# Order and engines of the last sums: an attention and gated feed-forward kernel on one core

## The chip, the cores and the metric

The kernel runs on one core of one Trainium2 chip. The metric is the device time of one execution in microseconds (us); a time is the median of several runs. The engines are named as in the profile: PE is TensorE (PEld its weight loads), DVE is VectorE, ACT is ScalarE, POOL is GpSimd and SP is SyncE, which issues most of the DMAs.

## The reference

Two blocks follow one another. The first is attention with a threshold: of each row of scores only those within `tau` of the row's maximum are kept. The second is a gated feed-forward block on the attention's output, with its heads put side by side. All data are float32.

```python
# q, k, v: (8, 8, 576, 64) = batch, heads, sequence, head size; tau = 0.02
scores = matmul(q, k^T) / sqrt(64)
scores = where(scores >= max(scores) - tau, scores, -1e9)
attn   = exp(scores - max(scores)); attn = attn / (sum(attn) + 1e-9)
x      = matmul(attn, v)            # -> (8 * 576 = 4608 tokens, 512)

# w_gate, w_val: (512, 1536); w_out: (1536, 512)
g   = x @ w_gate
out = (g * sigmoid(g) * (x @ w_val)) @ w_out
```

## The kernel before

**Work and stages.** The 64 pairs of batch and head are taken two heads at a time. From the second batch on, such a pair is a segment of three slots (`slot_scores`, `slot_rest`, L2042 and L2063). A slot computes 6 tiles of 128 x 288 scores, takes maxima, exponentials and masks with row sums, adds the halves of each sum (`exchange` on ACT, L2115; `total` on DVE, L2120 and L2121, which leaves the reciprocal `ri`), scales the six tiles (on ACT, L2133, or, for as many as the table `POOLED` says, on POOL, L2130) and transposes them (DVE, L2135). `attend` (L2141) multiplies a segment's three slots with the values (PE, L2157), one slot after the next segment begins. The feed-forward block runs on units of 512 tokens (one batch, of which 64 tokens per batch are put aside; those of all batches make up the last unit). In the code a unit is `c`, and `B` = 8: `c` = B - 1 is the last batch's unit, `c` = B that of the tokens put aside.

**Products by sums.** Every matrix product of the block is done by Strassen's scheme with seven products in place of eight, most of them nested twice. So each needs sums of its operands (`inner_sums`, `early`, `late`, `second_of_s1`: SBUF to SBUF, through `dve_tt`, L929, or `pool_tt`, L926) and sums of its results (`fold`, `folded`, `combine`, `add`).

**Behind the last scores.** Once the last slot is done, `tail[0]` is set and the kernel goes through four stages. (1) The rest of unit B - 2's output products (`px` and `py`, L1768), with the last `attend` between its fifth and sixth. (2) The gates: for each of six columns `g` and each of the units B - 1 and B one `Whole` (L2526) of seven products, `p1`, `p5`, the former one's `p4`, `p2`, `p6`, `p3`, `p7` (PE, L2543). Behind `p6` two fills copy a result from PSUM (ACT, L1271 and L1273); `p7` waits for them. Behind `p3` and `p7` DVE adds the results (L2615, L2625) and POOL folds them (`fold`, four instructions); `finish` takes the tanh of the fold (ACT, L2593), multiplies on DVE (L2595) and then on DVE or POOL. The next `p4` waits for L2625. (3) The output products of unit B - 1 (`Deep`): the steps `p1`, `gates_end` (the last `Whole`'s `p4`), `p2`, `p7_alone`, `p5_flat`, `p6_alone`, `p3_flat`, `p4_alone`. (4) Those of unit B: `p1`, `gates_end`, `p7_alone`, `p2`, and so on: here the seventh product stands ahead of the second. What stage (4) reads was stored in `hall_hbm` (L2608) and is loaded by four DMAs of SP (L2669).

**Sums around the change.** In `Deep`, `early` begins the sums `s3` and `s1` over the halves of the gated values; `second_of_s1` adds one more behind the last value of column 4; `late` adds the last of `s1` and the three of `s2`, each 128 x 512. `inner_sums(o, ...)` makes four sums of 128 x 384 for the nested product `o`: `o` = 1 is the second product's operand, 5 the sixth's, 6 the seventh's.

**What sets the order.** The order on each engine is fixed when the program is built, by a planner (`Plan`, L28). Every piece is a job with an engine, a cost in us, a rank and the jobs it depends on. `peek` (L60) takes the engine that can start first and, among the jobs that are ready there, the lowest rank, then the earliest ready:

```python
n = min((i for i, j in enumerate(jobs) if j.ready <= start + (0.0 if j.rank else self.PATIENCE)),
        key=lambda i: (self.rank(jobs[i], start), jobs[i].ready, i))
```

`PATIENCE` is 0.2 and holds for rank 0 alone; a job of rank 0 that is ready up to 0.2 later is taken before one of rank 1. `lag` is time between the end of a job on its engine and the moment its result counts as there. PE's products are issued in the order of the code.

Of the kernel before, what the change touches and what calls it, by code (L numbers as in the profile page):

```python
# [14 lines left out]
ALU = mybir.AluOpType  # L15
# [129 lines left out]
def kernel(  # L145
# [13 lines left out]
    B, H, S, D = q.shape  # L159
# [1101 lines left out]
    class Seven(Buf):  # L1261
# [13 lines left out]
        def fold(self, eng, rank, *deps):  # L1275

            y = self.place.rearrange("p (x q) -> p x q", q=P)
            tt, took, less = (dve_tt, 0.36, 0.23) if eng == "DVE" else (pool_tt, 0.85, 0.52) if tail[0] else (pool_tt, 0.75, 0.44)
            twice = lambda x: y[:, x:x + 1].broadcast_to((P, 2, P))
            j = job(eng, took, tt(y[:, 1:3], twice(0), y[:, 1:3], ALU.add), *deps, rank=rank)  # L1280
            j = job(eng, took, tt(y[:, 0:7:6], twice(2), y[:, 5:7], ALU.add), j, rank=rank)
            j = job(eng, less, tt(y[:, 2], y[:, 0], y[:, 3], ALU.add), j, rank=rank)
            return job(eng, took, tt(y[:, 4:6], twice(6), y[:, 4:6], ALU.add), j, rank=rank)

    class Flat:

# [388 lines left out]
    class Deep:  # L1675
# [37 lines left out]
            self.sixth_place = xall[:, 2 * KW:3 * KW]  # L1713
            self.sixth_sums(mark)

        by_pool = False

        def second_of_s1(self):
            self.by_pool = True
            x = NF2 // 2 - 2  # L1720
            self.ready["s1"].append(self.sum(self.a21, self.a21, self.a22, ALU.add, x, self.ready["s3"][x], gated[self.c, 1, NF2 - 2]))

# [10 lines left out]
        def sum(self, out, a, b, op, x, *deps, rank=2):  # L1733
            fs = slice(2 * x, 2 * x + 2)
            tt, eng, took = (dve_tt, "DVE", 0.62) if tail[0] else (pool_tt, "POOL", 1.3)
            rank = min(rank, 1) if tail[0] else rank
            if self.by_pool and not self.in_outputs:
                tt, eng, took = pool_tt, "POOL", 1.3
            return job(eng, took, tt(out[:, fs], a[:, fs], b[:, fs], op), *deps, rank=rank)

        def inner_sums(self, o, a, place, ready, *deps):

            a11, a21, a12, a22 = quarters(a)
            flat = place if len(place.shape) == 2 else place.rearrange("p f n -> p (f n)")
            s1, s2, s3, s4 = (flat[:, n * QW:(n + 1) * QW].rearrange("p (f q) -> p f q", q=P) for n in range(4))
            tt, eng, took = (dve_tt, "DVE", 0.55) if tail[0] else (pool_tt, "POOL", 1.0)
            rank = 0 if o == 1 and self.c == B - 1 else 0 if o == 1 else 1 if o == 5 or o in (3, 6) and not tail[0] or o in (0, 6) and tail[0] or self.c == B - 2 else 2
            j3 = job(eng, took, tt(s3, a11, a21, ALU.subtract), *ready, *deps, rank=rank)
            j1 = job(eng, took, tt(s1, a21, a22, ALU.add), *ready, *deps, j3, rank=rank)
            j2 = job(eng, took, tt(s2, s1, a11, ALU.subtract), j1, rank=rank)  # L1750
            j4 = job(eng, took, tt(s4, a12, s2, ALU.subtract), j2, rank=rank)
            self.inner[o] = [(a11, ready), (a12, ready), (s4, [j4]), (a22, ready), (s1, [j1]), (s2, [j2]), (s3, [j3])]
# [310 lines left out]
    def slot_rest(seg, t, pss, mark, pooled, max_by_act, rank):  # L2063
        m = 2 * NU3
        mx, nm, th, ri, tot = statistics("mx", "nm", "th", "ri", "tot")
        sm = sums[0]
        sums.rotate(1)
        old_sums, sum_users[0] = sum_users[0], []
        sum_users.rotate(-1)
        tiles = [(h, u) for u in range(NU3) for h in range(2)]  # L2070
        at_of = lambda h, u: seg["p"] + (2 * (NU3 * t + u) + h) * SH
        scs = {(h, u): pss[h][:, u, 0:SH] if u < 2 else pss[h][:, :, SH:SH + SQ] for h, u in tiles}
        flat = {x: pall[:, at_of(*x):at_of(*x) + SH] for x in tiles}
        ps = {x: y if x[1] < 2 else y.rearrange("p (a n) -> p a n", a=2) for x, y in flat.items()}
        n_of = lambda h, u: NU3 * h + u
        rs = []
        for h, tile_ in enumerate(pss):
            n = n_of(h, 0)
            rs.append(job("DVE", 0.72, lambda n=n, tile_=tile_: nc.vector.tensor_reduce(  # L2079
                out=mx[:, n:n + 2, 0], in_=tile_[:, :, 0:SH], axis=AX.X, op=ALU.max, negate=True), mark, rank=0))  # L2080
            rs.append(job("DVE", 0.42, lambda n=n, tile_=tile_: nc.vector.tensor_reduce(  # L2081
                out=mx[:, n + 2:n + 3, 0], in_=tile_[:, :, SH:SH + SQ], axis=AX.XY, op=ALU.max, negate=True), mark, rank=0))

        def largest():
            for g in range(NG):
                o = g ^ 1
                nc.vector.tensor_reduce(out=mx[g * G:(g + 1) * G, 0:m, 1], in_=mx[o * G:(o + 1) * G, 0:m, 0:1], axis=AX.X, op=ALU.max)
            nc.vector.tensor_reduce(out=nm[:, 0:m], in_=mx[:, 0:m, :], axis=AX.X, op=ALU.min)

        def others():  # L2090
            for g in range(NG):
                o = g ^ 1
                nc.scalar.copy(mx[g * G:(g + 1) * G, 0:m, 1], mx[o * G:(o + 1) * G, 0:m, 0])

        if max_by_act:
            oj = job("ACT", 0.78, others, *rs, rank=0)
            nj = job("DVE", 0.18, lambda: nc.vector.tensor_reduce(out=nm[:, 0:m], in_=mx[:, 0:m, :], axis=AX.X, op=ALU.min), oj, rank=0)
        else:
            nj = job("DVE", 0.82, largest, *rs, rank=0)
        ej = job("ACT", 0.25, lambda: nc.scalar.activation(th[:, 0:m], nm[:, 0:m], AF.Identity, bias=cut, scale=-1.0), nj, rank=0)  # L2100
        masks = {}
        for h, u in tiles:
            x, n = (h, u), n_of(h, u)
            ej = job("ACT", 0.42, lambda x=x, n=n: nc.scalar.activation(ps[x], scs[x], AF.Exp, bias=nm[:, n:n + 1]), ej,  # L2104
                     masks.get((h, u - 1)), rank=0)
            masks[x] = job("DVE", 0.45, lambda x=x, n=n: nc.vector.scalar_tensor_tensor(  # L2106
                out=ps[x], in0=scs[x], scalar=th[:, n:n + 1], in1=ps[x], op0=ALU.is_ge, op1=ALU.mult, accum_out=sm[:, n, 0:1]),
                ej, *old_sums, rank=0)
        sc_users[:] = masks.values()
        behind_scores[0] = rs[0]  # L2110

        def exchange():
            for g in range(NG):
                o = g ^ 1
                nc.scalar.copy(sm[g * G:(g + 1) * G, 0:m, 1], sm[o * G:(o + 1) * G, 0:m, 0])  # L2115

        xj = job("ACT", 0.78, exchange, *masks.values(), rank=1)

        def total():
            nc.vector.tensor_reduce(out=tot[:, 0:m], in_=sm[:, 0:m, :], axis=AX.X, op=ALU.add)  # L2120
            nc.vector.reciprocal(out=ri[:, 0:m], in_=tot[:, 0:m])  # L2121

        rj = job("DVE", 0.36, total, xj, rank=1)
        sum_users[-1].append(rj)
        for u in range(NU3):
            scaled = []
            for h in range(2):
                x, n = flat[h, u], n_of(h, u)
                if h and u < pooled:
                    scaled.append(job("POOL", 0.48 if seg["i"] >= 3 * NP else 0.4, lambda x=x, n=n: nc.gpsimd.tensor_scalar(  # L2130
                        out=x, in0=x, scalar1=ri[:, n:n + 1], scalar2=1.0, op0=ALU.mult, op1=ALU.mult), rj, rank=1))
                else:
                    scaled.append(job("ACT", 0.46, lambda x=x, n=n: nc.scalar.activation(x, x, AF.Copy, scale=ri[:, n:n + 1]), rj, rank=rank))  # L2133
            both = pall[:, at_of(0, u):at_of(0, u) + 2 * SH]
            seg["turned"].append(job("DVE", 0.72, lambda both=both: nc.vector.transpose(out=both, in_=both), *scaled, rank=rank))  # L2135
# [139 lines left out]
    GV = {1: 3, 2: 6, 3: 4, 4: 6, 5: 7, 6: 3, 7: 5, 8: 7, 9: 0}  # L2275
    GV_FIRST = {1: 5, 2: 8, 3: 2, 4: 5, 5: 7, 6: 2, 7: 5, 8: 7, 9: 0}
    CH = {0: 2, 1: 3, 10: 4, 11: 4}
    POOLED = {0: 3, 1: 1, 2: 1, 3: 3, 4: 3, 5: 2, 6: 1, 7: 2, 8: 1}
    MAX_BY_ACT = (0, 1, 3, 4, 5, 6, 8, 9)
    FIRST_POOLED = {0: 2, 4: 1, 5: 1, 8: 1, 9: 1, 11: 2, 12: 2, 13: 3, 15: 3, 16: 3, 17: 2, 19: 2, 20: 2, 22: 3, 23: 3}  # L2280
    FIRST_MAX_BY_ACT = (1, 3, 6, 9, 10, 11, 12, 13, 14, 18, 20, 21)
# [56 lines left out]
    for s, (n, x) in enumerate((n, x) for n in range(len(halved)) for x in range(NU3)):  # L2338
# [20 lines left out]
            store_last(0, j)  # L2359
        if s == 1:  # L2360
            prepare_v(seg)
        at_, pooled, max_by_act = (kk, POOLED, MAX_BY_ACT) if b > DEEP else (s, FIRST_POOLED, FIRST_MAX_BY_ACT)
        slot_rest(seg, t, pss, mark, pooled.get(at_, 0), at_ in max_by_act, 1 if x == NU3 - 1 else 2)
        if x == 1 and n > 0:
            for place, load in held:
# [270 lines left out]
    for g in range(NF2):  # L2636
        for c in (B - 1, B):
# [10 lines left out]
            for fn in (new.p2, new.p6, new.p3, new.p7) if old is not None else (new.p5, new.p2, new.p6, new.p3, new.p7):  # L2648
                fn()
                if (c, g) == (B, NF2 - 1) and fn == new.p2:  # L2650
                    state["deep"].sums_of_last(plan.t + plan.PIPE)
                if (c, g) == (B, NF2 - 1) and fn == new.p6:
                    state["deep"].late(plan.t + plan.PIPE)
            old = new
    state["last_product"] = old.p4
    begin_outputs(B - 1)
# [56 lines left out]
```

## Time and profile before

| | |
|---|---|
| median of 3 runs | 1343.5 us (1342.71 to 1345.19) |
| the profiled execution | 1344.29 us; its span, first to last instruction, 1342.4 us |
| PE | busy 1327.0 us (99%), granted clock 0.999 |
| DVE | busy 1082.9 us (81%) |
| ACT | busy 899.1 us (67%) |
| POOL | busy 932.8 us (69%) |
| last scores on PE | from 1110.45 us |
| last `attend` | from 1126.85 us |
| first product of the gates | from 1136.26 us |
| first output product of unit B - 1 | from 1267.05 us |
| first output product of unit B | from 1303.63 us |
| end of PE's last product, about | 1338.8 us |

In a timeline a row is: start, length, engine, line, operation, output from inputs with shapes, count, and in brackets the idle time of the engine before it and what released it. Rows of one line and shape that follow each other are merged, and an instruction's length includes what it waits for inside. In the view of waits a row is: who waited for whom, us in total, times, longest.

### The profile page before, as it was taken

The numbers are of one execution on the slowest core, as the hardware profiler recorded it, in microseconds if no ns is written. First come the engines' busy times: TensorE is split into PE (matmuls) and PEld (weight loads), VectorE is DVE, ScalarE is ACT, GpSimd is POOL, SyncE is SP. The second block draws the span as 40 slices with busy tenths as digits, with TensorE's granted clock in tenths as the row PEclk, the third lists the DMA queues.
The fourth block names the chain that finished last, engine by engine and source line by source line (L and its number), as shares of the span: only waits on it lengthen the run. The fifth ranks groups of instructions, "written<-read, shape, count | busy, mean of one in ns | idle before, by whom it ended". The sixth has DMA issues, their size and how long they took to land. (4 is left out here: it accounts for less than half of the span.)

```text
span 1342.4 us, 41686 instructions
## 1 busy us (share of the span) xinstructions
PE 1327.0 (99%) x16274; PEld 1123.1 (84%) x16274; DVE 1082.9 (81%) x2891; ACT 899.1 (67%) x2341; POOL 932.8 (69%) x1115
## 2 busy tenths in 40 slices
PE   9999999999999999999999999999999999999998
PEld 7777877787887878888888888888888889999998
DVE  7888898888887778888888887888888887667886
ACT  6888777767756677787777777777777775344300
POOL 2688497565685759857895779677976799856720
PEclk9999999999999999999999999999999999999999
DMA  8852424356557553656365746655474627565241
GB/s 180 205 188 92 85 58 134 122 150 178 154 166 220 174 167 89 208 165 219 76 201 168 232 111 187 178 168 149 115 214 146 213 68 232 158 202 183 88 169 40
DMA packets 230884, 209.81 MB, mean 156 GB/s; under 512 B 167968, under 2 KB 185376, under 8 KB 223008
## 3 DMA queue, kind: packets, MB, share of 16 engines
q1 hardware_dynamic: 226768, 206.22, 52.2%
q8 instruction: 129, 2.11, 0.7%
q10 hardware_dynamic: 3920, 0.92, 0.3%
q14 instruction: 67, 0.55, 0.1%
HBM read 169.08 MB, written 38.01 MB: 154 GB/s over the span
## 5 line engine op out<-in xcount | busy, mean ns | idle before, releaser
L2106 DVE SCALAR_TENSOR_TENSOR pall<-sc,th,pall 128x288 f32<-128x288 f32 x504 | 244.2, 513 | 42.6 <-ACT pall L2104 23.4
L2104 ACT ACTIVATE pall<-sc,nm 128x288 f32<-128x288 f32 x504 | 232.9, 498 | 35.3 <-DVE pall L2106 34.9
L2135 DVE STREAM_TRANSPOSE pall<-pall 128x576 f32<-128x576 f32 x252 | 188.3, 764 | 22.1 <-ACT pall L2133 12.1
L1138 PE MATMUL pb<-xall,big 128*128 128x256 f32 x864 | 205.8, 381 | 0.0
L2133 ACT ACTIVATE pall<-pall,ri 128x288 f32<-128x288 f32 x388 | 178.9, 527 | 27.7 <-DVE ri L2121 26.9
L926 POOL TENSOR_TENSOR big<-big 128x128 f32<-128x128 f32 (+3 forms) x214 | 158.9, 751 | 46.5 <-ACT big L1273 20.8
L1138 PEld LDWEIGHTS pb<-xall,big 128*128 128x128 f32 x864 | 161.2, 190 | 24.0 <-issue 2.2
L926 POOL TENSOR_TENSOR hall<-hall,tmp 128x512 f32<-128x512 f32 x80 | 102.3, 1279 | 95.6 <-DVE hall L1197 75.9
L2079 DVE TENSOR_REDUCE mx<-sc 128x2 f32<-128x576 f32 x168 | 125.7, 748 | 39.7 <-PE sc L2058 39.3
L2058 PE MATMUL sc<-kT,qT 64*32 64x288 f32 (+1 forms) x5376 | 145.3, 345 | 0.4 <-DVE pall L2106 0.4
L1138 PE MATMUL pa<-xall,big 128*128 128x256 f32 x576 | 137.7, 382 | 0.0
L2058 PEld LDWEIGHTS sc<-kT,qT 64*32 64x32 f32 x5376 | 96.2, 106 | 48.6 <-issue 9.3
L2157 PE MATMUL xa<-pall,vall 64*32 64x288 f32 x4032 | 129.4, 404 | 0.5 <-PE px L1768 0.4
L1138 PEld LDWEIGHTS pa<-xall,big 128*128 128x128 f32 x576 | 107.8, 190 | 17.5 <-issue 2.5
L2157 PEld LDWEIGHTS xa<-pall,vall 64*32 64x32 f32 x4032 | 75.6, 107 | 46.6 <-issue 5.0
L2130 POOL TENSOR_SCALAR pall<-pall,ri 128x288 f32<-128x288 f32 x116 | 58.2, 513 | 53.1 <-DVE ri L2121 52.8
L1138 PE MATMUL pe<-xall,big 128*128 128x256 f32 x384 | 91.4, 381 | 0.0
L2115 ACT COPY sums<-sums 32x6 f32<-32x6 f32 x336 | 66.6, 198 | 30.3 <-DVE pall L2106 25.2
L1138 PEld LDWEIGHTS pe<-xall,big 128*128 128x128 f32 x384 | 72.4, 190 | 11.1 <-ACT pall L2133 0.7
L2081 DVE TENSOR_REDUCE mx<-sc 128x1 f32<-128x288 f32 x168 | 75.0, 447 | 0.0
L926 POOL TENSOR_TENSOR hall<-hall 128x384 f32<-128x384 f32 (+2 forms) x69 | 70.0, 1028 | 0.8
L1196 ACT ACTIVATE vall<-tmp 128x512 f32<-128x512 f32 x72 | 45.1, 627 | 35.6 <-POOL tmp L926 19.0
(365 smaller groups left out, 3051.6 us busy)
## 6 DMA issues: line engine op xcount, KB each, us to landing
big<-sums_hbm SPq DMA_DIRECT2D x30, 1280.0 KB, 7.9
big<-sums_hbm SPq DMA_DIRECT2D x30, 1024.0 KB, 7.8
vall<-in_v_dram SPq DMA_DIRECT2D x112, 144.0 KB, 3.5
big<-sums_hbm SPq DMA_DIRECT2D x54, 256.0 KB, 3.6
sums_hbm<-big SPq DMA_DIRECT2D x36, 256.0 KB, 3.8
out_dram<-big SPq DMA_DIRECT2D x32, 256.0 KB, 2.8
qT<-in_q_dram SPq DMA_DIRECT2D x112, 72.0 KB, 4.0
kT<-in_k_dram SPq DMA_DIRECT2D x112, 72.0 KB, 3.0
```

The costliest lines, as they stand in the source:

```text
L926: return lambda: nc.gpsimd.tensor_tensor(out=out, in0=a, in1=b, op=op)
L1138: nc.tensor.matmul(ps[:, i], w[:, k_, i * P:(i + 1) * P], x[:, k_, :], start=first and i == k_ == 0, stop=True, skip_group_check=True)
L2058: nc.tensor.matmul(pss[h][(slice(g * G, (g + 1) * G), *part)], qT[hs, col:col + G], kT[hs, c * SH + keys[0]:c * SH + keys[1]], start=True, ...
L2079: rs.append(job("DVE", 0.72, lambda n=n, tile_=tile_: nc.vector.tensor_reduce(out=mx[:, n:n + 2, 0], in_=tile_[:, :, 0:SH], axis=AX.X, op= ...
L2081: rs.append(job("DVE", 0.42, lambda n=n, tile_=tile_: nc.vector.tensor_reduce(out=mx[:, n + 2:n + 3, 0], in_=tile_[:, :, SH:SH + SQ], axis ...
L2104: ej = job("ACT", 0.42, lambda x=x, n=n: nc.scalar.activation(ps[x], scs[x], AF.Exp, bias=nm[:, n:n + 1]), ej, masks.get((h, u - 1)), rank=0)
L2106: masks[x] = job("DVE", 0.45, lambda x=x, n=n: nc.vector.scalar_tensor_tensor(out=ps[x], in0=scs[x], scalar=th[:, n:n + 1], in1=ps[x], op0 ...
L2115: nc.scalar.copy(sm[g * G:(g + 1) * G, 0:m, 1], sm[o * G:(o + 1) * G, 0:m, 0])
L2130: scaled.append(job("POOL", 0.48 if seg["i"] >= 3 * NP else 0.4, lambda x=x, n=n: nc.gpsimd.tensor_scalar(out=x, in0=x, scalar1=ri[:, n:n ...
L2133: scaled.append(job("ACT", 0.46, lambda x=x, n=n: nc.scalar.activation(x, x, AF.Copy, scale=ri[:, n:n + 1]), rj, rank=rank))
L2135: seg["turned"].append(job("DVE", 0.72, lambda both=both: nc.vector.transpose(out=both, in_=both), *scaled, rank=rank))
L2157: nc.tensor.matmul(holds[a].ap()[x * G:(x + 1) * G, 0:SH].rearrange("d (i q) -> d i q", q=G), vr[rs, h, j, ds], p[rs, h, :, j, :], start=( ...
```

## The change

In the very last slot the exchange and the total get rank -1 in place of 1, and two of the six scales go to POOL in place of none (the table's new entry `NS`). A `fold` in the tail gets a lag of 0.6 in the planner. `second_of_s1` and the four sums of `late` for unit B - 1 go from POOL to DVE, and `late` is no longer called behind the last `Whole`'s `p6` but from `gates_end`, behind the last `p4`. For unit B the seventh product's sums get rank 0 in place of 1, and the second operand's sums rank 1 in place of 0.

```diff
@@ -1280,7 +1280,7 @@
             j = job(eng, took, tt(y[:, 1:3], twice(0), y[:, 1:3], ALU.add), *deps, rank=rank)
             j = job(eng, took, tt(y[:, 0:7:6], twice(2), y[:, 5:7], ALU.add), j, rank=rank)
             j = job(eng, less, tt(y[:, 2], y[:, 0], y[:, 3], ALU.add), j, rank=rank)
-            return job(eng, took, tt(y[:, 4:6], twice(6), y[:, 4:6], ALU.add), j, rank=rank)
+            return job(eng, took, tt(y[:, 4:6], twice(6), y[:, 4:6], ALU.add), j, rank=rank, lag=0.6 if tail[0] else 0.0)
 
     class Flat:
 
@@ -1713,10 +1713,7 @@
             self.sixth_place = xall[:, 2 * KW:3 * KW]
             self.sixth_sums(mark)
 
-        by_pool = False
-
         def second_of_s1(self):
-            self.by_pool = True
             x = NF2 // 2 - 2
             self.ready["s1"].append(self.sum(self.a21, self.a21, self.a22, ALU.add, x, self.ready["s3"][x], gated[self.c, 1, NF2 - 2]))
 
@@ -1734,8 +1731,6 @@
             fs = slice(2 * x, 2 * x + 2)
             tt, eng, took = (dve_tt, "DVE", 0.62) if tail[0] else (pool_tt, "POOL", 1.3)
             rank = min(rank, 1) if tail[0] else rank
-            if self.by_pool and not self.in_outputs:
-                tt, eng, took = pool_tt, "POOL", 1.3
             return job(eng, took, tt(out[:, fs], a[:, fs], b[:, fs], op), *deps, rank=rank)
 
         def inner_sums(self, o, a, place, ready, *deps):
@@ -1744,7 +1739,7 @@
             flat = place if len(place.shape) == 2 else place.rearrange("p f n -> p (f n)")
             s1, s2, s3, s4 = (flat[:, n * QW:(n + 1) * QW].rearrange("p (f q) -> p f q", q=P) for n in range(4))
             tt, eng, took = (dve_tt, "DVE", 0.55) if tail[0] else (pool_tt, "POOL", 1.0)
-            rank = 0 if o == 1 and self.c == B - 1 else 0 if o == 1 else 1 if o == 5 or o in (3, 6) and not tail[0] or o in (0, 6) and tail[0] or self.c == B - 2 else 2
+            rank = 0 if o == 6 and self.c == B else 0 if o == 1 and self.c == B - 1 else 1 if o == 1 and tail[0] else 0 if o == 1 else 1 if o == 5 or o in (3, 6) and not tail[0] or o in (0, 6) and tail[0] or self.c == B - 2 else 2
             j3 = job(eng, took, tt(s3, a11, a21, ALU.subtract), *ready, *deps, rank=rank)
             j1 = job(eng, took, tt(s1, a21, a22, ALU.add), *ready, *deps, j3, rank=rank)
             j2 = job(eng, took, tt(s2, s1, a11, ALU.subtract), j1, rank=rank)
@@ -2114,13 +2109,14 @@
                 o = g ^ 1
                 nc.scalar.copy(sm[g * G:(g + 1) * G, 0:m, 1], sm[o * G:(o + 1) * G, 0:m, 0])
 
-        xj = job("ACT", 0.78, exchange, *masks.values(), rank=1)
+        first = -1 if seg is halved[-1] and t == seg["tiles"][-1] else 1
+        xj = job("ACT", 0.78, exchange, *masks.values(), rank=first)
 
         def total():
             nc.vector.tensor_reduce(out=tot[:, 0:m], in_=sm[:, 0:m, :], axis=AX.X, op=ALU.add)
             nc.vector.reciprocal(out=ri[:, 0:m], in_=tot[:, 0:m])
 
-        rj = job("DVE", 0.36, total, xj, rank=1)
+        rj = job("DVE", 0.36, total, xj, rank=first)
         sum_users[-1].append(rj)
         for u in range(NU3):
             scaled = []
@@ -2275,7 +2271,7 @@
     GV = {1: 3, 2: 6, 3: 4, 4: 6, 5: 7, 6: 3, 7: 5, 8: 7, 9: 0}
     GV_FIRST = {1: 5, 2: 8, 3: 2, 4: 5, 5: 7, 6: 2, 7: 5, 8: 7, 9: 0}
     CH = {0: 2, 1: 3, 10: 4, 11: 4}
-    POOLED = {0: 3, 1: 1, 2: 1, 3: 3, 4: 3, 5: 2, 6: 1, 7: 2, 8: 1}
+    POOLED = {NS: 2, 0: 3, 1: 1, 2: 1, 3: 3, 4: 3, 5: 2, 6: 1, 7: 2, 8: 1}
     MAX_BY_ACT = (0, 1, 3, 4, 5, 6, 8, 9)
     FIRST_POOLED = {0: 2, 4: 1, 5: 1, 8: 1, 9: 1, 11: 2, 12: 2, 13: 3, 15: 3, 16: 3, 17: 2, 19: 2, 20: 2, 22: 3, 23: 3}
     FIRST_MAX_BY_ACT = (1, 3, 6, 9, 10, 11, 12, 13, 14, 18, 20, 21)
@@ -2359,7 +2355,7 @@
             store_last(0, j)
         if s == 1:
             prepare_v(seg)
-        at_, pooled, max_by_act = (kk, POOLED, MAX_BY_ACT) if b > DEEP else (s, FIRST_POOLED, FIRST_MAX_BY_ACT)
+        at_, pooled, max_by_act = (kk if n + 1 < len(halved) or x + 1 < NU3 else NS, POOLED, MAX_BY_ACT) if b > DEEP else (s, FIRST_POOLED, FIRST_MAX_BY_ACT)
         slot_rest(seg, t, pss, mark, pooled.get(at_, 0), at_ in max_by_act, 1 if x == NU3 - 1 else 2)
         if x == 1 and n > 0:
             for place, load in held:
@@ -2649,8 +2645,6 @@
                 fn()
                 if (c, g) == (B, NF2 - 1) and fn == new.p2:
                     state["deep"].sums_of_last(plan.t + plan.PIPE)
-                if (c, g) == (B, NF2 - 1) and fn == new.p6:
-                    state["deep"].late(plan.t + plan.PIPE)
             old = new
     state["last_product"] = old.p4
     begin_outputs(B - 1)
```

`gates_end` calls `late` itself where it hasn't been called yet (`if "s2" not in self.ready`), after the flag `in_outputs` is set.

## The prediction

> **What bounds the kernel now.** The page first: TensorE (PE) is busy 1327.0 of 1342.4 us, 99%, at a granted clock of 0.999, so only its waits can be won. The change begins in the last attention slot, whose scores start at 1110.45 us, and ends with the output stage, so I read the waits of PE by size and kept those after 1110:
>
> ```profile
> PE sc L2543 <- DVE tmp L2625: 0.9, 1, 0.9
> PE px L1768 <- DVE big L929: 0.9, 1, 0.9
> ...
> PE sc L2543 <- ACT tmp L1273: 0.5, 1, 0.5
> PE xa L2157 <- PE px L1768: 0.4, 1, 0.4
> ```
>
> In PE's timeline they lie at 1271.90 (0.94), 1312.34 (0.91), 1166.24 (0.53) and 1126.43 (0.42): 2.80 us, 0.21%. Two rows are stretched besides: six products of 0.96 at 1246.38 beside 0.83 elsewhere, and a pair of 0.49 at 1138.50 beside 0.39: 0.13 and 0.10. Nothing else in the changed stretch can be gained: 3.03 us. Then the timelines of the engines ahead of the four. ScalarE (ACT):
>
> ```profile
> 1120.53 0.83 ACT L2115 COPY sums<-sums 32x6 f32<-32x6 f32 x4 [0.59 <-DVE pall L2106]
> ...
> 1165.22 0.63 ACT L2593 ACTIVATE qT<-big 128x512 f32<-128x512 f32 x1 [1.81 <-POOL big L926]
> 1165.76 0.47 ACT L1271 ACTIVATE tmp<-sc 128x384 f32<-128x384 f32 x1
> 1166.13 0.59 ACT L1273 ACTIVATE tmp<-sc 128x512 f32<-128x512 f32 x1
> ```
>
> A tanh waits 1.81 us for a GpSimd (POOL) fold and holds up the two fills behind it, for which PE waits. VectorE (DVE):
>
> ```profile
> 1121.78 0.69 DVE L2018 TENSOR_TENSOR vall<-py,vall 128x512 f32<-128x512 f32 x1 [1.28 <-PE py L1768]
> ...
> 1122.85 0.16 DVE L2120 TENSOR_REDUCE tot<-sums 128x6 f32<-128x18 f32 x1
> ...
> 1263.75 1.65 DVE L929 TENSOR_TENSOR big<-hall 128x384 f32<-128x384 f32 x1
> ...
> 1270.15 1.57 DVE L929 TENSOR_TENSOR big<-hall,big 128x384 f32<-128x384 f32 x1
> 1271.65 1.14 DVE L2625 SCALAR_TENSOR_TENSOR tmp<-sc,tmp 128x512 f32<-128x512 f32 x2
> ...
> 1310.40 2.28 DVE L929 TENSOR_TENSOR xall<-xall 128x384 f32<-128x384 f32 x4
> ...
> 1312.80 0.55 DVE L929 TENSOR_TENSOR big<-big 128x384 f32<-128x384 f32 x1
> ```
>
> The total stands behind two adds; L2625, for which PE waits, behind sums that take 1.6 in place of 0.55; the seventh's last sum (1312.80) behind four of the second operand's. POOL, at the same time:
>
> ```profile
> 1263.72 2.81 POOL L926 TENSOR_TENSOR big<-hall,big 128x512 f32<-128x512 f32 x2
> ...
> 1273.80 1.58 POOL L926 TENSOR_TENSOR hall<-hall 128x512 f32<-128x512 f32 x1
> ```
>
> These, and another of 1.58 at 1275.34, are the late sums.
>
> **The change part by part.** *Exchange and total.* The exchange ends at 1121.36 and runs on an idle ACT, so its rank moves nothing. The total can then start at 1121.40, ahead of the adds (ready when py ends, 1121.74), and ri is there at 1121.8 instead of 1123.24. Two of six scales go to POOL; ACT's four take 4 x 0.445 = 1.8, to 1123.6. The adds end near 1122.9, the three transposes take 2.48 from there, to 1125.4 instead of 1126.74. PE is free for the attention at 1126.43: the wait of 0.42 goes, with a cover of 1.0. What is late next is 11 us on: the pair at 1138.50 takes its operand from a DVE step that ends at 1138.44, so this chain is without slack. It begins with the fold at 1129.65, behind POOL's 2.10 add, and no attention sets that. The two scales (0.51 each) push POOL by 1.03, of which 0.27 reaches that add, because now it waits for ACT until 1127.43. Against it, the chain stood still 0.46 before 1136.82 for PE's own product, which comes 0.42 earlier. Bounds for the whole part: a gain of 0.42 (the chain follows PE) and a loss of 0.3 (only the delay arrives); I take 0.42 - 0.27 = 0.15, since the idle row is the nearer one. POOL's sums for the third product shift by 1.03 too; they ended at 1125.99 and are read from 1131.47: covered.
>
> *Lag of 0.6 on folds.* It costs no instruction: it tells the planner that the fold's result comes later, so the tanh yields to what is ready sooner. At 1165.22 the fills become ready about 1164.3 and the tanh at 1165.2, so the fills go first: 0.53 gone. In the other passes the tanhs were ready when their turn came, and a pass leaves ACT idle 3.5 to 4.1 us before the L2557 copies, which covers 0.6 to 1.2 us of a later tanh. The stretched 0.96 follows an L2625/L2615 pair queued behind the product step at 1244.50 that the lag moves back: bounds 0 and 0.13; I take 0.1, as that step is 0.68 long. A new wait is possible where a fold comes sooner than the lag says: bound 0.5 (one tanh ahead of a fill), taken at 0, for only at 1252.80 do the two tie in the planner's costs.
>
> *Late sums by DVE.* Five sums of 128x512 leave POOL: that at 1249.79 (1.27), where DVE is idle from 1249.2 to 1250.5, and the four late ones. A DVE sum of this form takes 0.60 undisturbed (two start at 1282.17, the next instruction at 1283.37), so 4 x 0.60 = 2.4 on DVE, issued only after the last gate product. In return DVE's own sums get free of the four on POOL. Undisturbed they take 0.55 (hall<-hall, four at 1286 to 1290); beside the four they took 1.65 and 1.09, 1.51 and 1.51: 3.6 over. Of this, 1.6 lies ahead of L2625, which then starts at 1271.65 - 1.6 = 1270.05; PE asks for it at 1271.90: the wait of 0.94 goes, cover 0.7. On POOL only folds and one product were queued behind the four, and they start sooner. On DVE the sixth product's sums are queued behind them: the balance there is 2.4 - 2.0 = +0.4. Their last is ready at 1286.20 and read six steps of 0.67 after 1289.07, at 1293.1; with PE 1.7 early a cover of 5 us is left. The bound upwards: each DVE sum also waits out one POOL fold step of 0.72, 2.9 more.
>
> [...]
>
> *Second operand behind the seventh's.* The four sums of 2.28 leave the front of 1312.80, so it ends by 1311.1 instead of 1313.35. PE, 1.7 us early by the parts above, asks at 1310.6: by rank alone 0.5 would stay. But DVE sat idle 5.86 us up to 1295.74 for hall_hbm, whose loads SyncE (SP) issues at 1289.26, behind an output store that waits for a DVE fold (1288.24). The last product that they read, POOL's at 1284.20, comes some 4 us sooner when POOL has no late sums ahead of it. In the planner's costs two of them (1.3 each) stand there, and the loads are issued 1.0 behind the output store; taken 2.4 forward they are issued ahead of it. So the 0.91 goes: bounds 0.4 and 0.91, I take 0.91. The second operand's sums are read from 1314.2 on, over 4.7 us: covered by about 2 us.
>
> Sum: 0.15 + 0.53 + 0.1 + 0.94 + 0.91 = 2.63. The profiled execution took 1344.29 (span 1342.4 and 1.9 around it), 0.8 over the median of 1343.5, so 1341.7 for it and **1340.9** for the median.
>
> **The rivals.** (a) *One wait stays or comes back*: DVE sums blocked by folds keep L2625 late, or the chain at 1138.5 takes back more than 0.42, or a tanh holds a fill. For it: covers of 0.7 and none. Price 0.5 to 1: 1341.6 to 1341.9, say 1341.7.
> (b) *Everything goes, the 0.42 too*: 3.0 at most, 1340.5. Against it: the 0.27 from POOL.
> (c) *Slower: VectorE's output stage becomes the bound.* DVE is busy 17.54 of 18 us from 1272 to 1290. If all four sums meet folds and nothing is freed, 2.4 + 2.9 = 5.3 are added ahead of the fold at 1288.15, and if the loads stay behind its store they go out at 1294.6. The seventh's last sum then ends at 1311.1 + 5.3 = 1316.4, while PE comes at 1310.6: a wait of 5.8 in place of 0.91, against 1.72 won before: 1343.5 + 4.9 - 1.7 = 1346.7. It decides from 2.1 us of added DVE time. Against it: the freed 2.0 and the earlier load.
> (d) *The first part does not do what it says*: rank decides only between jobs that are ready together, and total and adds are ready 0.3 apart; the order then stays and 0.15 is lost: 1341.1, inside the forecast.
>
> **How the numbers follow.** Forecast with (d) 0.60, (a) 0.17, (b) 0.12, (c) 0.11. Runs of before spread over 2.5 us, so about 0.2%, 2.7 us, is what a measurement of this kernel can tell from no change; that mark is 1340.8, just under the forecast. Of the forecast's 0.60 I count 0.36 beyond it (over half, since what the freed engines shorten elsewhere is not in the sum), all 0.12 of (b), none of (a): faster 0.48, slower 0.11, and 0.41 within. The range reaches from 1340.0 ((b) less half a microsecond of spread) to 1343.0 ((a) at its upper price and 1.1 of spread); it leaves out (c) and little else.
>
> **What would show it.** Right: no wait of PE over 0.2 us at xa L2157, at L2543 and at px L1768; the total (L2120) ahead of L2018; L1271 ahead of the qT tanh near 1165; 128x512 sums hall<-hall on DVE after 1273 and none on POOL; the loads from hall_hbm issued before 1285. The first part is wrong if sc<-xall near 1138 isn't stretched by 0.2 or more. The whole is wrong if the sums on DVE average over 1 us and PE waits for px in the last unit, or if a new wait over 1 us stands between 1136 and 1267.

## The result and the profile after

The changed kernel took 1348.2 us in the median of nine executions (1343.56 to 1349.57), the kernel before 1344.04 beside it: a ratio of 1.0028, 95% interval 1.002 to 1.0037. It lies 7.3 us above the forecast of 1340.9 and 5.2 us above the range, on the slow side. How the executions spread belongs to the finding: those at 1343.56 and 1344.58 had a mean granted clock of 0.999 or more, the other seven 0.996 to 0.998. The trace is of the quickest (span 1341.8, clock 1.000). Its lines are some 4 to 5 lower in number than those of before.

The view of PE's waits from 1110 us on, as shown of before:

```profile
PE px L1763 <- DVE xall L929: 2.3, 1, 2.3
PE pa L2539 <- ACT pb L2553: 1.4, 1, 1.4
```

All four old waits are gone, and two new ones, both longer than any of the old, stand in their place. First what went as planned. DVE's timeline at the last slot, then ACT's at 1165, then DVE's at the end of the gates:

```profile
1120.04 0.17 DVE L2116 TENSOR_REDUCE tot<-sums 128x6 f32<-128x18 f32 x1 [0.89 <-ACT sums L2110]
...
1120.43 0.69 DVE L2013 TENSOR_TENSOR vall<-py,vall 128x512 f32<-128x512 f32 x1
```

```profile
1164.68 0.49 ACT L1271 ACTIVATE tmp<-sc 128x384 f32<-128x384 f32 x1 [1.35 <-PE sc L2539]
1165.06 0.59 ACT L1273 ACTIVATE tmp<-sc 128x512 f32<-128x512 f32 x1
1165.54 0.63 ACT L2589 ACTIVATE qT<-big 128x512 f32<-128x512 f32 x1
```

```profile
1264.29 0.55 DVE L929 TENSOR_TENSOR big<-hall 128x384 f32<-128x384 f32 x1
...
1267.71 1.57 DVE L929 TENSOR_TENSOR big<-big,hall 128x384 f32<-128x384 f32 x1
1269.21 1.14 DVE L2621 SCALAR_TENSOR_TENSOR tmp<-sc,tmp 128x512 f32<-128x512 f32 x2
```

The total runs ahead of the adds, the fills ahead of the tanh, and the sum that took 1.65 beside POOL's late sums takes 0.55. Now the two new waits. The first, in the timelines of SP, DVE, ACT and PE in turn:

```profile
1129.19 0.37 SPq L2395 DMA_DIRECT2D pall<-last_hbm  x1
1129.60 1.09 SPq L1252 DMA_DIRECT2D big<-sums_hbm  x1
1130.73 0.43 SPq L1256 DMA_DIRECT2D big<-sums_hbm  x1
1131.21 0.43 SPq L1252 DMA_DIRECT2D big<-sums_hbm  x1
1131.68 0.43 SPq L1258 DMA_DIRECT2D big<-more_hbm  x1
1132.21 0.90 SPq L1824 DMA_DIRECT2D out_dram<-big  x2
```

```profile
1137.31 1.72 DVE L929 TENSOR_TENSOR big<-big,px 128x256 f32<-128x256 f32 x4 [0.61 <-DMA out_dram<-big]
```

```profile
1138.69 0.95 ACT L2553 COPY pb<-pa 128x512 f32<-128x512 f32 x2 [3.84 <-DVE big L929]
```

```profile
1139.31 0.71 PE L2539 MATMUL pa<-xall,big 128*128 128x128 f32 x4 [1.39 <-ACT pb L2553]
```

Read from the last line up: PE waits for a copy of ACT, the copy for DVE's combination of unit B - 2's third product, and this for the landing of an earlier output store, whose block it overwrites. SP issued that store behind a load of the last unit's operand (`last_hbm`), which it had to hold until the attention was done, and behind four loads of cells for the gates (`load_cell`). Before, the order was the other one:

```profile
1130.94 1.72 SPq L1829 DMA_DIRECT2D out_dram<-big  x2
1132.76 0.41 SPq L2399 DMA_DIRECT2D pall<-last_hbm  x1
1133.22 0.49 SPq L1252 DMA_DIRECT2D big<-sums_hbm  x1
```

No line of the diff names these DMAs. In the planner's costs the attention's end came 0.95 sooner (the first part's own gain), so the loads that it releases became ready at 1007.54 in place of 1008.49; the two stores are ready at 1008.36 and 1008.91 (before: 1007.95 and 1008.15). The planner gives SP what can start first: the loads passed the stores.

The second, in DVE's timeline and PE's:

```profile
1278.58 2.97 DVE L929 TENSOR_TENSOR big<-hall,big 128x512 f32<-128x512 f32 x3
1281.47 1.64 DVE L929 TENSOR_TENSOR big<-big,px 128x256 f32<-128x256 f32 x4
1283.02 0.55 DVE L929 TENSOR_TENSOR xall<-big,xall 128x384 f32<-128x384 f32 x1
```

```profile
1283.63 0.94 PE L1763 MATMUL px<-extra,xall 128*128 128x128 f32 x6 [2.32 <-DVE xall L929]
```

The sum at 1283.02 is the last of the four for unit B - 1's seventh product. Three late sums, and a combination that became due meanwhile, stand ahead of it on DVE. In the planner's costs both have rank 1; the late sums are ready at 1149.62, the seventh's last at 1149.68.

### The profile page after: what moved, and what is told of

It is laid out like the page before. It is cut to its first block, busy times and chain, and to the rows that moved or that the text cites. A ratio compares the mean times of both kernels' runs of the same rounds, so it can differ in the third digit from the quotient of the medians.

```text
span 1341.8 us, 41659 instructions
## 1 busy us (share of the span) xinstructions
PE 1326.0 (99%) x16274; PEld 1121.2 (84%) x16274; DVE 1089.2 (81%) x2896; ACT 898.2 (67%) x2339; POOL 930.1 (69%) x1112
## 4 chain that ended last, share of the span: by engine, by line
PE 92%; DVE 4%; DMA 1%; POOL 1%; issue 0%; ACT 0%; SPq 0%; ACTq 0%; DVEq 0%; POOLq 0%
PE pb L1138 14%; PE px L1763 11%; PE sc L2053 10%; PE pa L1138 10%; PE xa L2153 9%; PE pe L1138 6%; PE po L1446 6%; PE sc L2539 5%; PE py L1763 3%; PE pe L1333 3%; PE pb L2539 3%; PE pg L1371 2%; PE pv L1371 2%; PE pa L2539 2%; PE py L1772 2%; PE sc L484 1%
## 5 line engine op out<-in xcount | busy, mean ns | idle before, releaser
L2053 PE MATMUL sc<-kT,qT 64*32 64x288 f32 (+1 forms) x5376 | 144.8, 345 | 0.0
L2053 PEld LDWEIGHTS sc<-kT,qT 64*32 64x32 f32 x5376 | 96.0, 106 | 48.2 <-issue 9.3
L926 POOL TENSOR_TENSOR tmp<-tmp 128x256 f32<-128x256 f32 (+3 forms) x53 | 51.3, 978 | 29.0 <-DVE tmp L2611 11.8
```

The lines of the kernel that those rows point to most:

```text
L926: return lambda: nc.gpsimd.tensor_tensor(out=out, in0=a, in1=b, op=op)
L2053: nc.tensor.matmul(pss[h][(slice(g * G, (g + 1) * G), *part)], qT[hs, col:col + G], kT[hs, c * SH + keys[0]:c * SH + keys[1]], start=True, ...
```

## The experiments

Theories at the start: T1, the pause at 1283 costs its 2.3 us and is followed by a low clock; T2, the pause at 1139 is the one that does this; T3, the low clock has nothing to do with the change. Then, for the cause of the first pause: P1, SP's order; P2, GpSimd made later by the two scales. The common measure is the stretch on PE from the start of the last scores (L2053; L2058 in before) to the start of its last group of products (L1772; L1777), in the profiled execution: it leaves out the start of the kernel, where executions differ by up to 3 us. "Lost to clock" is the sum of one minus the granted clock over windows of 1 us in that stretch. A pause here is a wait of PE over 1 us; shorter waits aren't in the table.

| kernel | pause at 1139 | pause at 1283 | lost to clock | stretch | median us (runs) | ratio, 95% |
|---|---|---|---|---|---|---|
| before | none | none | 0 | 222.98 | | |
| after | 1.39 | 2.32 | 0 | 223.67 | 1348.20 (9) | 1.0028 (1.002 to 1.0037) |
| after_again | 2.38 | 2.31 | 1.70 + 1.71 | 227.67 | 1349.29 (5) | 1.004 (1.0028 to 1.0052) |
| late_behind | 3.2 | none | 1.70 | 225.45 | 1347.26 (11) | 1.0022 (1.0012 to 1.0033) |
| no_pool_scales | 2.5 | 2.33 | 1.71 | 226.12 | 1345.82 (12) | 1.0019 (1.0009 to 1.0028) |
| late_behind_no_pool | 1.5 | none | 0 | 221.77 | 1344.27 (11) | 1.0003 (0.9994 to 1.0012) |
| loads_behind | none | 2.3 | 0 | 222.60 | 1344.74 (11) | 1.0005 (0.9996 to 1.0014) |
| mended_a | none | none | 0 | 220.92 | 1341.31 (11) | 0.9978 (0.9969 to 0.9987) |
| mended_b | none | none | 0 | 221.14 | 1341.88 (11) | 0.9982 (0.9973 to 0.999) |
| before_loads_ahead | none | none | 0 | 222.50 | 1344.11 (11) | 1.0 (0.9992 to 1.0009) |
| before_last_ahead | 2.3 | none | 0 | 225.87 | 1348.41 (11) | 1.0023 (1.0013 to 1.0032) |
| slot_only | 3.39 | none | 3.41 | 228.72 | 1349.14 (5) | 1.0033 (1.0021 to 1.0045) |
| late_only | none | 3.37 | 3.41 | 228.06 | 1348.46 (7) | 1.003 (1.0019 to 1.0042) |
| lag_and_swap | none | none | 0 | 221.69 | 1343.01 (11) | 0.999 (0.9982 to 0.9999) |

For the changed kernel the stretch adds up: before without its 3.03 us of waits is 219.95; with the two new pauses that is 223.66, and after shows 223.67.

**after_again**: the changed kernel unaltered.

> The changed kernel once more, to have a profile of one of its longer executions. T1 (the 2.32 us pause of TensorE before unit B-1's seventh product, at 1283.6, is followed by a granted clock below 1 for some 10 us): about 1347 to 1349 in most executions, 1343.5 in the others; in a longer one the two new pauses of 1.4 and 2.3 us are no longer than in a shorter one, and the granted clock is below 1 behind 1283 and 1.00 everywhere else. T2 (the 1.39 us pause at 1139 does it): the same times, but the clock is low behind 1139. T3 (no pause does it; the lower clock stands anywhere, at the start too): the low clock is in a stretch that the change doesn't touch, before 1110.

Measured 1349.29. Its profiled execution is a long one (clock 0.997). The windows of 1 us show where (columns: window, length, PE's busy time and count, granted clock, DMA share, GB/s):

```profile
1139.00:1140.00 1.00, 0.00 (x0) 1.00 0.21 55
1140.00:1141.00 1.00, 0.00 (x0) 0.85 0.02 5
1141.00:1142.00 1.00, 0.72 (x3) 0.50 0.05 18
1142.00:1143.00 1.00, 1.00 (x7) 0.50 0.71 244
1143.00:1144.00 1.00, 1.00 (x7) 0.50 0.00 0
1144.00:1145.00 1.00, 1.00 (x10) 0.95 0.00 0
```

```profile
1287.00:1288.00 1.00, 1.00 (x7) 0.73 0.66 220
1288.00:1289.00 1.00, 1.00 (x4) 0.50 0.89 263
1289.00:1290.00 1.00, 1.00 (x3) 0.50 1.23 249
1290.00:1291.00 1.00, 1.00 (x4) 0.56 0.98 250
```

At each pause the clock falls to a half for 3.4 us; behind the first, PE issues 7 instructions in 1 us where it issues 12 at a clock of 1.00 (each window from 1146 to 1155). By the windows that is 1.7 us each time. The stretch is longer by a little less, 3.0 us for both, once 0.99 for the longer first pause is taken off: the first low clock begins near 1140.7, still inside the pause, where it costs nothing. Up to PE's last product the clock is 1.00 everywhere else in this execution, so T3 falls for it, and T1 and T2 are both right, each for its own pause. The first pause is also not of fixed length: 2.38 here, 1.39 in the other execution.

T3 isn't wholly wrong for the other kernels: seven of the fourteen profiled executions have a half clock of 3.4 us (1.70 or 1.71 lost) near 8 or 118 us, far ahead of the change. Neither after nor after_again has one, but a low mean clock alone doesn't say that one of the two pauses made it.

**late_behind**: unit B - 1's late sums made to wait for the seventh's last sum (`mark` becomes `*mark` in the sums of `s2` too).

```diff
-            self.ready["s1"].append(self.sum(self.a21, self.a21, self.a22, ALU.add, n - 1, j3[n - 1], gated[c, 1, NF2 - 1], rank=1))
+            mark = [mark, *(self.inner[6][2][1] if c == B - 1 else ())]
+            self.ready["s1"].append(self.sum(self.a21, self.a21, self.a22, ALU.add, n - 1, j3[n - 1], gated[c, 1, NF2 - 1], *mark, rank=1))
```

> The changed kernel, with the three late sums of unit B-1 made to wait for the last of the sums for its seventh product, so that they stand behind them on VectorE. T1: the 2.32 us pause goes, the granted clock is 0.999 or more in all executions, and the median falls by 6 to 7 us from the changed kernel's (4.5 of clock and 2.3 of pause), to 1341 to 1342. T2: the pause goes and 2.3 us with it, but most executions still have a clock of 0.996 to 0.998: median 1345 to 1346. T3: as T2.

1347.26, above T1's figure and T2's too. The pause at 1283 and the low clock behind it are gone; the one at 1139 is there, 3.2 us long in this execution, with 1.70 of clock behind it. T1 alone doesn't explain the median.

**no_pool_scales**: the table's entry `NS: 2` taken out.

> The changed kernel with all six scales of the very last slot on ScalarE instead of two on GpSimd. The 1.39 us pause at 1139 goes, since GpSimd's combination starts a microsecond earlier; ScalarE's last scale ends 1 us later, of which up to 0.5 may show before the transposes. T1: the 2.3 us pause stays and most executions still have the lower clock: median 1346 to 1348. T2: the clock is 0.999 or more in all executions: median 1342 to 1343. T3: as T1, 1346 to 1348.

1345.82, just under the figure of T1. The pause that was to go stayed:

```profile
PE pa L2539 <- ACT pb L2553: 2.5, 1, 2.5
PE px L1763 <- DVE xall L929: 2.3, 1, 2.3
```

So my reading of its cause, GpSimd started later by two scales, was wrong, and P2 with it. SP's order here is that of the changed kernel.

**late_behind_no_pool**: both.

> Both edits together: no pause of TensorE over 1 us is left between 1110 and the outputs. T1 and T2: clock 0.999 or more in all executions, median 1339.5 to 1341 (the 2.6 us of waits of the kernel before are gone and the 3.7 of new ones too). T3: 1344 to 1345.5 with most executions at the lower clock.

1344.27: no better than before. The pause at 1139 is left, 1.5 us in the profiled execution, and three of the eleven have a clock of 0.997. The profiled stretch is still 1.21 shorter than before's; this execution lost 1.71 us of clock between 8 and 12 us, ahead of the stretch, so the median isn't fully accounted for. It is T3's figure, but the pause that was to be gone wasn't.

**loads_behind**: the cell loads planned 1.5 us later, so that the stores come first again.

```diff
-    state["free_cells"](attended)
+    state["free_cells"](attended + 1.5)
```

> The changed kernel, with the loads of the last cells given a time 1.5 us later in the planner, so that SP issues the stores of the output blocks of unit B-2 ahead of them again, as in the kernel before. P1 (the pause at 1139 comes from SP's order: four loads ahead of the store whose landing VectorE's combination waits for): the pause falls from 1.4 to 3.2 us to 0.5 at most, the clock is 1.00 in the stretch 1140 to 1150, and the pause of 2.3 us at 1283 stays: median 1345 to 1346.5. P2 (it comes from GpSimd's combination, which two scales of the last slot make later): the pause stays at 1.4 us or more, median 1347.5 to 1349.5.

```profile
PE px L1763 <- DVE xall L929: 2.3, 1, 2.3
PE sc L2539 <- DVE xall L929: 0.2, 1, 0.2
```

The pause at 1139 is gone with the two scales still on POOL: P1. The median, 1344.74, is a quarter of a microsecond better than the expected range. How the store's landing changes is in the view of the tensor `out_dram`, whose line gives the time from issue to landing in us, min, median and max, of the two stores; first before, then after_again, then loads_behind:

```profile
DMA to landing us min/median/max: 2.2/2.2/2.2
```

```profile
DMA to landing us min/median/max: 5.2/5.3/5.4
```

```profile
DMA to landing us min/median/max: 2.2/2.5/2.7
```

Four loads of 256 KB are 1.05 MB; at the 366 to 380 GB/s that the DMAs moved from 1136 to 1138 in after_again they take 2.8 us by estimate, and the landing is later by 3.0 to 3.2: about what it takes if the store's bytes go out behind the loads'. The delay isn't fixed, though: the two stores took 4.3 to 4.5 us in after, where the pause is 1.39, and 5.9 to 6.2 in before_last_ahead below.

**mended_a**: both orders mended, the two scales left on POOL.

> The changed kernel with both orders mended: the cell loads behind the stores on SP, and unit B-1's late sums behind the sums for its seventh product on VectorE. P1: no wait of TensorE over 0.8 us is left between 1110 and 1335 and the granted clock is 0.999 or more in nearly all executions: 1340.5 to 1342, that is 2 to 3.5 us under the kernel before, about the sum of the four old waits. P2: the pause at 1139 and its low clock stay: 1344.5 to 1347.

```profile
PE py L1773 <- ACT pall L1786: 0.7, 1, 0.7
PE sc L2540 <- DVE xall L929: 0.2, 1, 0.2
```

1341.31, ratio 0.9978: faster than both kernels, as P1 had it. **mended_b** gives the seventh's sums rank 0 instead of the dependency (`o == 6 and self.c >= B - 1`):

> The changed kernel with both orders mended, the one on VectorE in another way: the sums for unit B-1's seventh product get rank 0 instead of the late sums a dependency. As with the dependency no wait over 1 us is left behind 1110: 1340.5 to 1342. If the earlier seventh's sums delay the folds or the sixth product's sums by more than their cover, a wait of 0.3 to 1 us shows before pb or sc: 1341.5 to 1343.

1341.88. It lacks the 0.7 at py and has 0.4 at sc behind L2621 and 0.2 at py instead; the two can't be told apart by time.

**before_loads_ahead**: in the kernel before the cell loads alone go ahead (`attended - 1.0`).

> The kernel before with one thing changed: the same cell loads given a time 1 us earlier in the planner, so that SP issues them ahead of the two stores; nothing else of the change is in it. P1: a pause of 1 to 3 us on pa appears near 1138 to 1141, TensorE's granted clock falls below 1 behind it in part of the executions: median 1345.5 to 1347.5. P2: no pause, median 1343.5 to 1344.5.

1344.11, no pause: P1 as I had put it missed. The landing did grow, to 5.0 to 5.7, but SP had issued the last of the four loads by 1130.40 (not by 1129.75, as the next expectation has it) and the first store at 1131.78, so it landed in time; the load of the last unit's operand, for which SP has to hold, stood behind the stores. **before_last_ahead** moves that load too:

```diff
-    load_last(1, 1, attended)
-    state["free_cells"](attended)
+    load_last(1, 1, attended - 1.0)
+    state["free_cells"](attended - 1.0)
```

> The kernel before with SP's order near 1130 as in the changed kernel, and nothing else of the change: both the load of the last scores' operand and the four cell loads get a time 1 us earlier, so that this load, which has to wait on SP for the end of the attention, stands ahead of the cell loads, and these ahead of the two stores. P1, sharpened after the run in which the cell loads alone went ahead and nothing was lost (there SP had issued them by 1129.75, before the store was due): the pause of 1 to 3 us on pa appears near 1139, the time from issue to landing of the stores grows from 2.2 us to 4 to 5.5 us, median 1345 to 1347. If SP's order isn't enough by itself: no pause, 1343.5 to 1344.5.

```profile
1127.17 5.32 SPq L2399 DMA_DIRECT2D pall<-last_hbm  x2
1132.53 0.61 SPq L1252 DMA_DIRECT2D big<-sums_hbm  x1
...
1134.67 0.90 SPq L1829 DMA_DIRECT2D out_dram<-big  x2
```

```profile
1140.71 0.42 DVE L929 TENSOR_TENSOR big<-big,px 128x256 f32<-128x256 f32 x1 [3.32 <-DMA out_dram<-big]
```

1348.41, an order on SP and nothing else. The four loads' bytes alone did nothing as long as they were issued early; with the held load in front, which keeps them back until the stores are due, the pause is there. Here it holds up a step of DVE that PE needs for `sc`, not the copy for `pa`, because DVE's order is another one. The held load alone in front did no harm: that is the order of loads_behind, where SP issued it at 1130.47 and the stores from 1132.56, which landed 2.2 and 2.7 us later. The median lies above the expected 1347; of the 4.2 us that the profiled execution takes over before's, 2.9 are in the stretch, 2.3 of these in a pause of PE that this combination ends, and 1.0 ahead of it, where no cause is shown.

**slot_only**: the first part alone on the kernel before.

> The kernel before with the first part alone: exchange and total of the very last slot first in rank, and two of its scales on GpSimd. In the planner the attention's end comes 0.95 us earlier by it, and SP's order near 1130 becomes: load of the last scores' operand, four cell loads, then the two stores. P1: the 0.42 us wait before the transposes is gone, but a pause of 1.4 to 3.2 us stands before pa near 1139, with a granted clock below 1 behind it where it is over 2 us: median 1345 to 1347.5, slower than the kernel before by 1 to 3.5 us. If the first part is worth what the forecast gave it (0.15 us, with bounds -0.3 and +0.42): 1343.5 to 1344.5.

```profile
PE pa L2544 <- ACT pb L2558: 3.4, 1, 3.4
PE sc L2544 <- DVE tmp L2626: 0.9, 1, 0.9
PE px L1768 <- DVE big L929: 0.8, 1, 0.8
PE sc L2544 <- ACT tmp L1273: 0.5, 1, 0.5
```

1349.14: the part that I had put at a gain of 0.15 loses 4.8 us alone by the medians (interval 2.8 to 6.0). The wait at xa is gone, as forecast; the three others of before are still there; from 1140.4, within the pause of 3.39, the clock is a half for 6.8 us (3.41 lost).

**late_only**: of the third part, the move of the sums to DVE, alone on the kernel before; `late` is still called behind `p6`.

> The kernel before with the third part alone: the late sums on VectorE at rank 1 instead of on GpSimd. In the planner's order they then stand ahead of the second and third of the sums for unit B-1's seventh product, and so does a combination. If what is queued behind them decides, the seventh product waits 3 to 8 us near 1282, the granted clock falls to a half behind it for 3 to 4 us in most executions, and the median is 1347 to 1353. If instead the cover of 5 us that the forecast gave to VectorE's queue holds, the 0.94 us wait for the rows of p4 is gone and the median is 1342.5 to 1343.5.

```profile
PE px L1763 <- DVE xall L929: 3.4, 1, 3.4
PE sc L2538 <- ACT tmp L1273: 0.5, 1, 0.5
```

1348.46, with a clock of 0.996 to 0.998 in all seven executions. The 0.94 for L2625 is gone as forecast, and 3.4 for the seventh came in its place; a wait of 0.50 at pb (1255.06), for a fill behind a tanh, is new too. As the call wasn't moved, this isn't the whole third part.

**lag_and_swap**: the second and fourth parts alone.

> The kernel before with the second and fourth parts alone: the lag of 0.6 us on the last sum of a fold, and the ranks of the second and the seventh product's sums exchanged for the last unit. Neither touches SP's order at 1130 or VectorE's order at 1283. The 0.53 us wait behind tanh at 1166 and the 0.91 us wait of the last unit's seventh product at 1312 are gone, the 0.42 and the 0.94 us stay: 1342.5 to 1343.5 and no pause over 1 us. A rival: one of the two waits is replaced by another of its size, 1344 to 1344.5.

```profile
PE sc L2543 <- DVE tmp L2625: 1.4, 1, 1.4
PE xa L2157 <- PE px L1768: 0.4, 1, 0.4
```

1343.01, ratio 0.999 (0.9982 to 0.9999). The 0.53 and the 0.91 are gone; L2625 didn't move, so PE, half a microsecond earlier, waits 1.4 for it in place of 0.94.

## Why the prediction was wrong, point by point

**What bounds the kernel**: right. PE's waits make the time: waits, lost clock and the 219.95 that is left give the stretches above to 0.4 us, in before_last_ahead to 0.7. What it lacked is that a wait can cost more than its length, when the clock falls at it: the two pauses of after_again cost 3.0 us beyond theirs. What the miss of 7.3 us is made of, as an estimate from two profiled executions: the forecast of 1340.9 and the two new pauses of after, 3.7, give 1344.6, about the two quick executions; the low clock of after_again adds 3.0 to 3.4, which gives 1347.6 to 1348.0.

**First part: the step that failed.** The wait of 0.42 went and the total moved ahead, against rival (d). But "what is late next is 11 us on" looked at DVE, ACT and POOL and not at SP, though the part moves the end of `attend`, and with it, in the planner, the release of a held load and of four cell loads on a queue with two stores. Bounds of +0.42 and -0.3 were worked out for the wrong chain; alone the part costs 4.8 us. The sign that the text set, "if a new wait over 1 us stands between 1136 and 1267", came true at 1139.31. POOL's 1.03 was priced about right, at 0.27: counted from the start of the last scores, the pair `sc<-xall` that was forecast to feel it starts at 27.66 in after and at 27.46 in no_pool_scales. Where SP's order is mended (mended_a) the pair starts at 27.78, against 28.05 in before: a gain of 0.27, where 0.15 was forecast.

**Second part**: right. 0.53 went in every kernel that has the lag. The stretched row stayed (0.97 at 1245.50), so 0.1 less. No tie at 1252.80 showed.

**Third part: the second step that failed.** L2625's wait of 0.94 went, by the 1.6 us freed ahead of it, as worked out. The step "on DVE the sixth product's sums are queued behind them" is the miss: unit B - 1's seventh product's last sum is queued there too and is read first. In before it ended at 1277.34 and was read from 1281.21, a cover of 3.9 us; in after it ended at 1283.57. The term was mis-sized as well: four late sums took 1.22 + 2.97 = 4.19 in place of 2.4, so 1.05 each, over the 1 us that the text had named as a sign. For the seventh's four sums, 4.56 in before's rows became 3.39, so the balance behind L2625 is near +3.0, not +0.4. The upper bound that I had set beside it, one POOL fold step of 0.72 for each sum, 2.9 in all, would have made it +3.3; the long rows, 1.22 at 1271.75 and 2.97 for three from 1278.58, lie beside POOL's 3.90 at 1271.38 and 1.58 at 1278.81, and I had gone by the shorter rows. By that arithmetic 2.6 us less on DVE would also have removed the wait of 2.32; that is argued and wasn't run.

**Fourth part**: right in what it gained, not in the way. The loads from `hall_hbm` were issued from 1284.13, DVE waited 0.92 for them in place of 5.86, and the 0.91 was gone. But they weren't issued ahead of the output store, as the text had it: the store went first, at 1283.13 in place of 1288.26, because the combination that it waits for ended at 1283.11 in place of 1288.23. It is the combination that stands ahead of the seventh's last sum in the second pause.

**The sum** of 2.63 was of the right size for what the four parts do once no order is spoilt: mended_a's stretch is 2.06 shorter than before's, and a new wait at py takes another 0.66; its median is 2.9 us under that of before (interval 1.7 to 4.2).

**The rivals.** (c), the only slower one, named DVE's output stage, which is the engine and the stage of the second pause, but for unit B's seventh product instead of unit B - 1's, and at 0.11; it also needed the loads from `hall_hbm` to stay late, and they didn't. Rival (a) did name the chain at 1138.5, but by POOL and at 1 us at most. None priced SP's order at that place, or the clock.

## What to carry to other kernels

When an edit moves the end of a step, list everything that this end releases, loads on a shared queue included, and what stands on that queue within a microsecond of them; a planner that orders by the earliest start can turn a gain of a microsecond into another order on an engine that the edit never names. A held load with only the stores behind it did no harm here (loads_behind: landing in 2.2 to 2.7 us), nor did four loads ahead of the stores that were issued early (before_loads_ahead: 5.0 to 5.7 us, no pause); the two together did (before_last_ahead: 5.9 to 6.2 us and a pause of 2.3). So look at what follows a held load in the queue and who waits for the last of these to land. And a few tenths of a percent in the mean granted clock are worth locating in windows of 1 us: here that named the two pauses at once.

## What the hardware showed

The granted clock has two values in these traces, 1.00 and 0.50 (a window of 1 us that holds a change lies between), and what is lost to it before PE's last product comes in portions: 1.70 or 1.71 us, a half of 3.4 us, and twice that. Of the pauses behind 1110 none of the three of 1.4 and 1.5 us (one in lag_and_swap) was followed by a low clock, three of seven of 2.3 to 2.5 us were, and all three of 3.2 to 3.4, two of them by a double portion. So the same program, with the same pause of 2.3 us, lost 1.7 us of clock in one execution and none in another; the wide spread of the changed kernel, 1343.56 to 1349.57, fits that. Ahead of 1110 a portion stands behind the wait at 8 us in the four executions where this is 1.91 to 2.22 us long and in none of the ten where it is 1.02 to 1.8. Three have one near 118 us, behind a wait of only 1.05 to 1.07 at 116 us; the other eleven have that wait too, 1.03 to 1.08 long, and no low clock. So the length of one pause alone doesn't decide. What else does is not shown by any run here.
